# Four small copies per score tile made by ScalarE instead of VectorE, in a kernel whose order a planner writes

## The chip, the cores and the metric

The kernel runs on one core of one Trainium2 chip. The metric is the device time of one launch in microseconds (us). Engines are named as the profile names them: PE is TensorE (PEld its weight load), DVE is VectorE, ACT is ScalarE, POOL is GpSimd, SP is SyncE, which here only issues DMAs.

## What is computed

Attention with pooled queries (4 batches, 8 heads, 1152 keys of 64 values, queries averaged in pairs to 576), and behind it two gated products over 2304 tokens. Everything is float32 at the boundary, the weights come as float64.

```python
def _attn_ref(q, k, v):
    q_pool = q.reshape(B, H, S // factor, factor, D).mean(axis=3)
    scores = scale * np.matmul(q_pool, k.transpose(0, 1, 3, 2))
    scores = scores - np.max(scores, axis=-1, keepdims=True)
    attn = np.exp(scores)
    attn = attn / (np.sum(attn, axis=-1, keepdims=True) + 1e-09)
    return np.matmul(attn, v).astype(np.float32)

def _moe_ref(x, w_in, w_out):              # 512 -> 2048 -> 512
    h = x @ w_in
    return (np.maximum(0.01 * h, h) @ w_out).astype(np.float32)

def _moe2_ref(x, w1, w2, w3, w_out):       # 512 -> 768 (three times) -> 512
    h = np.maximum(np.maximum(x @ w1, x @ w2), x @ w3)
    return (h @ w_out).astype(np.float32)
```

## The kernel before

The program has three stretches. The attention of batch 0 runs first, by one method (`attention`). The attention of batches 1 to 3 runs by another (`attention2`), while PE also does the two products ("experts") of the batch before. When the last attention is done, the experts of batch 3 run alone, together with the 64 tokens of each batch that were set aside.

**A score tile of `attention2`** (`scores2`, L721) holds 64 queries of two heads against all 1152 keys. Each batch has 4 pairs of heads and 9 tiles per pair, so 36 tiles per batch and 108 in all. The keys of one query are cut into quarters: 32 queries sit on 32 partitions four times, so that each quarter of the partitions holds half of the keys of one half of the queries. For one tile there stand in order:

- PE: 16 matmuls into the PSUM tile `s` (the trace has 32 records for them). There is one such tile and one buffer for it, so the next tile's matmuls wait until the last reader of this one is done.
- DVE, L749: one reduce over the tile, which leaves the negated maxima of each partition's keys in two spare columns of `s`.
- L718, in `meet_halves`: four copies of 32 partitions by 2 columns, PSUM to PSUM, that put beside each quarter's maxima those of the quarter that holds the other half of its keys. **These are what the change moves.**
- DVE, L719: a reduce over the two columns, which gives `z`, the joint negated maximum.
- ACT, L752: two exponentials of 576 columns with `z` as bias and their sums accumulated (each with a small accumulator read behind it). They are the last readers of `s`.
- DVE, L756: a transpose in blocks of 32 into `pt`, which the matmuls with the values (`pw`, issued in `values2`, 72 for one half of a pair) read later.

**Other work on the same engines.** PE's expert matmuls write `m` (128x512) and `o` (128x256). ACT takes results out of PSUM (L1107, L1119, L1135, L1157), rounds to the first of two float32r parts (L1042, L826), and while batch 1 runs it also decodes the float64 weights (L963, L966, then L982 to split them); DVE joins the decoded halves (L967), makes parts (L1108) and sums (L1121) and maxima (L1137). POOL makes second parts. The weights are decoded once, in the time of batch 1, and written to DRAM; later batches load them ready.

**What sets the order.** The Python code issues everything in one rough order. Then `plan` (L1172) replays it: it groups instructions into nodes (a score tile's 16 matmuls are one), gives each a `busy` time (how long its engine is taken) and a `late` time (until a reader may start), and walks forward by a list schedule, always taking the node that can begin first. A backward pass sets priorities, up to three times. The order found for each engine is written into the program as fixed; each engine then runs its list strictly in that order. The cost of ACT's nodes, which the change leaves alone, is

```python
late = 185 + 0.8 * cols + 190 * (len(i.outs) > 1) + ...
busy = late - 105
```

with `cols` the columns of the output; a copy of 2 columns is so planned with 82 ns of ACT's time. On DVE a copy of 2 columns was planned with 155 - 80 = 75 ns. Between two nodes of one engine the plan before lets the second start when the first's `busy` time is over, even where it reads the first's result.

Of the kernel before, what the change touches and what calls it, by code (L numbers as in the profile page):

```python
# [23 lines left out]
def kernel(  # L24
# [21 lines left out]
    nc = tc.nc  # L46
# [12 lines left out]
    X0 = 320  # L59
# [655 lines left out]
    def meet_halves(st, z):  # L715
        for c in range(4):
            d = c + 1 - 2 * (c % 2)
            nc.vector.tensor_copy(out=st[32 * c:32 * c + 32, :, 1], in_=st[32 * d:32 * d + 32, :, 0])  # L718
        nc.vector.tensor_reduce(out=z, in_=st, axis=AX.X, op=ALU.min)  # L719

    def scores2(n, ph, i):  # L721
# [271 lines left out]
    ready = set()  # L993
# [51 lines left out]
    class Main:  # L1045
        n = TM
# [11 lines left out]
    class Rest:  # L1058
        n = TR_
# [107 lines left out]
    SEM = 35  # L1167
# [4 lines left out]
    def plan():  # L1172
# [21 lines left out]
        def meet(x, y):  # L1194
            return any(a < d and c < b for a, b in x[2] for c, d in y[2])
# [13 lines left out]
        nodes = []  # L1209
        node_of = {}  # L1210
        for i in todo:
            e = name_of(i.engine)
            key = units.get(i.name)
            out = next((n for n, _ in accesses(i.outs)), None)
# [5 lines left out]
            node_of[i.name] = len(nodes) - 1  # L1220
        count = len(nodes)
        before = [set() for _ in nodes]
        users = {}
        wrote, read = {}, {}
        for n, node in enumerate(nodes):
            for i in node["ins"]:
                for args, others in ((i.ins, (wrote,)), (i.outs, (wrote, read))):
                    for t, ap in accesses(args):
                        users.setdefault(t, set()).add(n)
                        r = region(ap)  # L1230
                        for kind in others:
                            for m, q in kind.get(t, ()):
                                if m != n and m not in before[n] and (nodes[m]["e"] == node["e"] or meet(q, r)):
                                    before[n].add(m)
                        if slots[t][0][0].startswith("ps_") and kind is not None:
                            lo, hi = min(a for a, _ in r[2]) // 512, (max(b for _, b in r[2]) - 1) // 512
                            for m, q in (*read.get(t, ()), *wrote.get(t, ())):
                                if m != n and any(
                                    a // 512 <= hi and lo <= (b - 1) // 512 for a, b in q[2]
                                ):  # L1240
                                    before[n].add(m)
                for args, kind in ((i.ins, read), (i.outs, wrote)):
                    for t, ap in accesses(args):
                        r = region(ap)
                        kind.setdefault(t, []).append((n, r))
# [6 lines left out]
        for n, node in enumerate(nodes):  # L1252
            busy = late = move = 0.0
            for i in node["ins"]:
                outs = [ap for _, ap in accesses(i.outs)]
                cols = size(outs[0].ap) if outs else 512
                op, e = i.opcode, node["e"]
                kind = node["out"].rsplit("_", 1)[0] if node["out"] else ""
                if e == "PE":
                    if kind == "pv":  # L1260
                        one = cols / 1.2
                    elif kind == "pw" and cols >= X0 - 64:
                        one = (cols + 32) / 2.4
                    elif kind == "pw":
                        one = cols / 2.4
                    elif kind == "s" and cols == KQ:
                        one = cols / 4.8
                    elif kind in ("pst", "psf", "psk", "psr"):
                        one = 108.0
                    elif kind == "psq":  # L1270
                        one = max(cols, 64) / 1.2
                    else:
                        one = (cols + 32) / 2.4
                    if n < wide_at:
                        one *= 1.065
                    busy += one * 1.015
                    late = busy + 165
                elif e == "SP":
                    busy = 60.0
                    dst = i.outs[0].bass_ap  # L1280
                    move = size([(0, 1)] + [tuple(x) for x in dst.ap]) * 4 / 330.0
                    if tuple(dst.ap[-1]) == (1, 32):
                        move, busy = 2 * move, 2500.0
                    late = 3000 + move
                elif e == "Activation":
                    late = 185 + 0.8 * cols + 190 * (len(i.outs) > 1) + 180 * (kind[0] == "q" or kind == "kspare") + 100 * (kind == "q") + 85 * (kind in ("wraw", "wsplit"))
                    busy = late - 105
                elif e == "DVE":
                    if op == "TensorReduce":
                        cols = size(next(ap for _, ap in accesses(i.ins)).ap)  # L1290
                    psum = any(slots[t][0][0].startswith("ps_") for t, _ in accesses(i.ins))
                    two = len(list(accesses(i.ins))) > 1 and kind != "p"
                    slow = psum or two or op in ("TensorReduce", "StreamTranspose")
                    late = max(155, 110 + (1.13 if slow else 0.62) * cols + 190 * (kind[0] == "q"))
                    busy = late - 80
                else:
                    late = max(185, 130 + 2.3 * cols)
                    busy = late + 40
            inside = not any(slots[t][0][0].startswith("ps_") for t, _ in accesses(i.ins))
            node["shut"] = node["e"] in ("DVE", "Pool") and inside and i.opcode in (  # L1300
                "TensorTensor", "TensorCopy", "TensorScalarPtr"
            )
            node["busy"], node["late"], node["move"] = busy, late, move
            kind = node["out"].rsplit("_", 1)[0] if node["out"] else ""
            node["mode"] = {"pv": 1, "psz": 1, "pw": 3 * (cols < X0 - 64)}.get(kind, 2 * (kind == "s" and cols == KQ))
# [33 lines left out]
        def lag(n, m):  # L1339
            x, y = nodes[n], nodes[m]  # L1340
            if x["e"] == y["e"]:
                return x["busy"]
            return (3000 + x["move"] if x["move"] else x["late"]) + SEM

        def forward(prio):
# [6 lines left out]
            ready = [0.0] * count  # L1352
# [7 lines left out]
            for _ in range(count):  # L1360
                best = None
                for e in ENGINES:
                    for n in pool[e]:
                        t = max(ready[n], free[e])
                        if nodes[n]["shut"]:
                            t = max(t, shut)
# [50 lines left out]
                        narrow[k] -= 1  # L1417
                        narrow_at[k] = max(narrow_at[k], until[x])
                for m in after[n]:
                    ready[m] = max(ready[m], end + SEM if nodes[m]["e"] != e else t + node["busy"])  # L1420
                    waiting[m] -= 1
                    if not waiting[m]:
                        pool[nodes[m]["e"]].append(m)
# [136 lines left out]
```

## Time and profile before

| what | value |
|---|---|
| device time, median of 3 runs | 1176.5 us (1173.85 to 1178.46) |
| span of the profiled execution, first to last instruction | 1176.8 us |
| stretches of it | attention of batch 0: 0 to 175; batch 1: 175 to 431; batch 2: 431 to 676; batch 3: 676 to 917; join: 917 to 946; experts of batch 3: 946 to 1177 |
| busy in the span | PE 1124.3, DVE 687.6, ACT 541.2, POOL 323.9 us |

The page gives no device time of its own for the profiled execution; its span lies inside the range of the three runs and 0.3 us above their median, so the span is taken as its time. Busy time counts an engine as busy while any instruction of it runs. PE's is a modelled end, so what matters there are the pieces in which it has nothing and waits for another engine.

### The profile page before, as it was taken

The page shows a single profiled execution, that of the slowest core. Times are in us where ns is not written, and L with a number is a line of the kernel's source. Part 1 is how long each engine was busy: PE and PEld are TensorE (multiplying, and loading weights), DVE is VectorE, ACT ScalarE, POOL GpSimd, SP SyncE. Part 2 cuts the span into 40 slices and gives each one's busy share as a digit, 9 for nine tenths or more (in the row PEclk, how much of TensorE's full clock was granted, in tenths as well). Part 3 has the DMA queues.
Part 4 walks back from the last instruction along what each step waited for, and adds up shares of the span by engine and source line. Part 5 has one row for each costly group of instructions (what it writes and reads, how often), then busy time and mean ns, then how long its engine had stood idle before and what let it go on. Part 6 is the DMA issues. An engine that isn't in the chain of part 4 may idle for free. (4 is left out here: it accounts for less than half of the span.)

```text
span 1176.8 us, 28179 instructions
## 1 busy us (share of the span) xinstructions
PE 1124.3 (96%) x11684; PEld 876.7 (75%) x11684; DVE 687.6 (58%) x1412; ACT 541.2 (46%) x1203; POOL 323.9 (28%) x300
## 2 busy tenths in 40 slices
PE   6899999999999899999999989999999999999998
PEld 5566766767767676777777767767677888888898
DVE  5777527888787765776667565875776412222110
ACT  5888788767778633333333333333343221112111
POOL 1111046555554412222311121224111122223110
PEclk9999999999999999999999999999999999999999
DMA  5522069688887976565745483745534533333333
GB/s 171 135 65 66 3 223 308 194 267 274 261 282 225 250 188 175 149 173 144 196 136 164 120 218 121 179 148 147 168 123 146 165 133 127 126 126 123 109 129 105
DMA packets 154875, 193.09 MB, mean 164 GB/s; under 512 B 85500, under 2 KB 115964, under 8 KB 154748
## 3 DMA queue, kind: packets, MB, share of 16 engines
q1 hardware_dynamic: 154748, 191.30, 54.5%
q8 instruction: 92, 1.51, 0.5%
q14 instruction: 35, 0.29, 0.1%
HBM read 153.88 MB, written 35.13 MB: 161 GB/s over the span
## 5 line engine op out<-in xcount | busy, mean ns | idle before, releaser
L136 PE MATMUL m<-x,w 128*128 128x512 f32 x1224 | 293.6, 393 | 0.0
L752 ACT ACTIVATE p<-s,z 128x576 f32<-128x576 f32 x216 | 158.4, 739 | 241.4 <-DVE z L719 200.8
L136 PEld LDWEIGHTS m<-x,w 128*128 128x128 f32 x1224 | 225.3, 188 | 56.2 <-issue 10.2
L756 DVE STREAM_TRANSPOSE pt<-p 128x1152 f32<-128x1152 f32 x108 | 148.7, 1377 | 94.9 <-ACT p L752 94.6
L136 PE MATMUL s<-kt,q 64*32 64x288 f32 (+1 forms) x3568 | 165.0, 408 | 22.3 <-ACT p L752 15.9
L749 DVE TENSOR_REDUCE s<-s 128x2 f32<-128x1152 f32 x108 | 147.6, 1366 | 54.9 <-PE s L136 52.4
L136 PE MATMUL m<-g,w 128*128 128x512 f32 x576 | 141.7, 395 | 1.2 <-POOL g L1109 1.2
L136 PEld LDWEIGHTS s<-kt,q 64*32 64x32 f32 (+1 forms) x3568 | 74.4, 109 | 81.9 <-ACT p L752 37.0
L1109 POOL TENSOR_TENSOR g<-t,g 128x512 fp32r<-128x512 f32 x64 | 85.2, 1333 | 173.1 <-DVE g L1108 170.8
L136 PEld LDWEIGHTS m<-g,w 128*128 128x128 f32 x576 | 104.9, 188 | 30.4 <-issue 6.5
L136 PE MATMUL pw<-pt,v 64*64 64x160 f32 (+1 forms) x3456 | 112.2, 284 | 2.5 <-issue 2.5
L136 PEld LDWEIGHTS pw<-pt,v 64*64 64x64 f32 x3456 | 105.5, 133 | 12.1 <-issue 8.9
L136 PE MATMUL m<-x,wsplit 128*128 128x512 f32 x408 | 103.8, 403 | 0.7 <-ACT t L1135 0.4
L1107 ACT ACTIVATE t<-m 128x512 f32<-128x512 f32 x80 | 44.1, 555 | 120.8 <-PE m L136 113.9
L983 POOL TENSOR_TENSOR wsplit<-wraw,wsplit 128x512 fp32r<-128x512 f32 x56 | 74.2, 1330 | 74.1 <-ACT wsplit L982 48.0
L136 PEld LDWEIGHTS m<-x,wsplit 128*128 128x128 f32 x408 | 75.1, 191 | 23.8 <-issue 6.9
L718 DVE COPY s<-s 32x2 f32<-32x2 f32 x432 | 73.0, 169 | 14.9
L136 PEld LDWEIGHTS m<-pt,w 128*128 128x128 f32 x600 | 76.3, 188 | 4.6 <-DMA pt<-xr 1.0
L136 PE MATMUL m<-pt,w 128*128 128x256 f32 x600 | 77.6, 281 | 1.1 <-DMA pt<-xr 0.6
L1137 DVE TENSOR_TENSOR t<-m,t 128x512 f32<-128x512 f32 (+1 forms) x60 | 37.8, 630 | 69.2 <-PE m L136 69.2
L1108 DVE CAST g<-t 128x512 fp32r<-128x512 f32 x64 | 30.5, 481 | 73.3 <-ACT t L1107 73.2
L780 POOL TENSOR_TENSOR rd<-rh,fold 128x640 fp32r<-128x640 f32 (+1 forms) x24 | 29.9, 1246 | 138.4 <-DVE rh L777 131.2
(142 smaller groups left out, 1372.7 us busy)
## 6 DMA issues: line engine op xcount, KB each, us to landing
w<-w SPq DMA_DIRECT2D x168, 512.0 KB, 3.5
w<-wsplit SPq DMA_DIRECT2D x56, 512.0 KB, 6.0
wraw<-in_moe_w_out_dram SPq DMA_DIRECT2D x22, 512.0 KB, 5.7
wraw<-in_moe_w_dram SPq DMA_DIRECT2D x18, 512.0 KB, 5.3
v<-in_v_dram SPq DMA_DIRECT2D x32, 288.0 KB, 4.4
wraw<-in_moe_w_in_dram SPq DMA_DIRECT2D x16, 512.0 KB, 6.5
v<-in_v_dram SPq DMA_DIRECT2D x10, 576.0 KB, 8.0
qraw<-in_q_dram SPq DMA_DIRECT2D x32, 144.0 KB, 4.5
```

Source lines behind the costliest of these rows:

```text
L136: mm = f(*args, **kwargs)
L718: nc.vector.tensor_copy(out=st[32 * c:32 * c + 32, :, 1], in_=st[32 * d:32 * d + 32, :, 0])
L749: nc.vector.tensor_reduce(out=st[:, :, 0], in_=every, axis=AX.XY, op=ALU.max, negate=True)
L752: nc.scalar.activation(out=p[:, 2 * h:2 * h + 2], in_=ps[h][:, :, 0:KQ], func=ACTF.Exp, bias=z[:, h:h + 1], accum_out=rs[:, h, i:i + 1],)
L756: nc.vector.transpose(out=pt[:, :, i].rearrange("p m h j -> p h m j"), in_=p.rearrange("p (h x) (m i) -> p h (x m) i", h=2, m=KT),)
L780: nc.gpsimd.tensor_tensor(out=rd.rearrange("p (u j) -> p u j", j=nj), in0=rh.bitcast(F32).unsqueeze(2).to_broadcast([128, nu, nj]), in1=se ...
L983: nc.gpsimd.tensor_tensor(out=t[:, 1], in0=r, in1=t[:, 0], op=ALU.subtract)
L1107: nc.scalar.activation(out=t, in_=ps[:, 0:k.n], func=ACTF.Prelu, alpha=0.01)
L1108: nc.vector.tensor_copy(out=gt[:, 0], in_=t)
L1109: nc.gpsimd.tensor_tensor(out=gt[:, 1], in0=t, in1=gt[:, 0], op=ALU.subtract)
L1137: nc.vector.tensor_tensor(out=t, in0=ps[:, 0:k.n], in1=t, op=ALU.max)
```

## The change

In `meet_halves` the four copies are issued to ACT. In the planner four things differ: (a) two nodes of one engine other than PE, of which the second reads what the first wrote, are now `chained`: the second starts only when the first's `late` time and the 35 ns of a semaphore are over; (b) DVE's `late` and `busy` are altered a little, and nodes under 16 columns take 85 ns; (c) the narrow matmuls with the values take 58 or 66.5 ns each (before: 53.3 and 66.7); (d) a price of 200 ns for copies into `s` stands in DVE's branch, where after the change no such copy is left. All 11684 matmuls and all other instructions are the same; their order is planned anew on all engines.

```diff
     def meet_halves(st, z):
         for c in range(4):
             d = c + 1 - 2 * (c % 2)
-            nc.vector.tensor_copy(out=st[32 * c:32 * c + 32, :, 1], in_=st[32 * d:32 * d + 32, :, 0])
+            nc.scalar.copy(out=st[32 * c:32 * c + 32, :, 1], in_=st[32 * d:32 * d + 32, :, 0])
         nc.vector.tensor_reduce(out=z, in_=st, axis=AX.X, op=ALU.min)
...
+                                if args is i.ins and m != n and nodes[m]["e"] == node["e"] != "PE" and meet(q, r):
+                                    chained.add((m, n))
...
                     elif kind == "pw":
-                        one = cols / 2.4
+                        one = (58.0 if cols < X0 // 2 else 66.5)
...
-                    late = max(155, 110 + (1.13 if slow else 0.62) * cols + 190 * (kind[0] == "q"))
-                    busy = late - 80
+                    late = max(160, 110 + (1.09 if slow else 0.62) * cols + 190 * (kind[0] == "q"))
+                    busy = late - 78
+                    if kind == "s" and op == "TensorCopy":
+                        busy = 200.0
+                    elif cols < 16:
+                        busy = 85.0
...
             if x["e"] == y["e"]:
-                return x["busy"]
+                return x["late"] + SEM if (n, m) in chained else x["busy"]
...
-                    ready[m] = max(ready[m], end + SEM if nodes[m]["e"] != e else t + node["busy"])
+                    ready[m] = max(ready[m], end + SEM if nodes[m]["e"] != e or (n, m) in chained else t + node["busy"])
```

The lists of the two programs, engine by engine, show what the new plan does. First PE, in the first part of batch 2: what stands between one score tile (`s`) and the next. `m` are expert matmuls of 512 columns. Before:

```order
L136 MATMUL s<-kt,q 32x288 x16
L136 MATMUL m<-g,w 128x512 x18
L136 MATMUL s<-kt,q 32x288 x16
L136 MATMUL m<-g,w 128x512 x15
L136 MATMUL m<-x,w 128x512 x3
L136 MATMUL s<-kt,q 32x288 x16
```

After:

```order
L136 MATMUL s<-kt,q 32x288 x16
L136 MATMUL m<-x,w 128x512 x21
L136 MATMUL s<-kt,q 32x288 x16
L136 MATMUL m<-g,w 128x512 x18
L136 MATMUL s<-kt,q 32x288 x16
L136 MATMUL m<-g,w 128x512 x21
L136 MATMUL s<-kt,q 32x288 x16
```

Where 18 matmuls stood between two tiles there are now mostly 21.

Next DVE, at neighbouring places of batch 2: one tile before,

```order
L749 TENSOR_REDUCE s<-s 128x2
L718 COPY s<-s 32x2 x4
L719 TENSOR_REDUCE z<-s 128x2
L1121 TENSOR_TENSOR acc<-m,acc 128x512
L756 STREAM_TRANSPOSE pt<-p 128x2x18x32
L1121 TENSOR_TENSOR acc<-m,acc 128x512
```

and two tiles after:

```order
L749 TENSOR_REDUCE s<-s 128x2
L666 STREAM_TRANSPOSE qt<-qraw 128x576
L719 TENSOR_REDUCE z<-s 128x2
L825 TENSOR_TENSOR xf<-pw,rz 128x5x32 x2
L663 STREAM_TRANSPOSE kt<-kraw 128x1152
L756 STREAM_TRANSPOSE pt<-p 128x2x18x32
L1137 TENSOR_TENSOR t<-m,t 128x512
L749 TENSOR_REDUCE s<-s 128x2
L719 TENSOR_REDUCE z<-s 128x2
```

The copies are gone from DVE's list; in their place stands nothing (45 of the 108 tiles) or other work, which `z` then stands behind.

Last ACT, in batch 1, where the weights are decoded. Before:

```order
L752 ACTIVATE p,sums<-s,z 128x576 x2
L982 CAST wsplit<-wraw 128x512
L963 ACTIVATE wraw<-wraw 128x512
L966 ACTIVATE wraw<-wraw 128x512
L982 CAST wsplit<-wraw 128x512
L963 ACTIVATE wraw<-wraw 128x512
L966 ACTIVATE wraw<-wraw 128x512
L752 ACTIVATE p,sums<-s,z 128x576 x2
```

After:

```order
L718 COPY s<-s 32x2 x4
L1107 ACTIVATE t<-m 128x512
L982 CAST wsplit<-wraw 128x512
L752 ACTIVATE p,sums<-s,z 128x576 x2
L963 ACTIVATE wraw<-wraw 128x512
L1107 ACTIVATE t<-m 128x512
L982 CAST wsplit<-wraw 128x512
L966 ACTIVATE wraw<-wraw 128x512
L963 ACTIVATE wraw<-wraw 128x512
L966 ACTIVATE wraw<-wraw 128x512
L718 COPY s<-s 32x2 x4
L752 ACTIVATE p,sums<-s,z 128x576 x2
```

ACT now has two places in each tile's chain, and its other work is planned between them, on either side.

## Rows read from the trace of the kernel before

**Rows 1.** The page: busy time by engine, and the granted TensorE clock in 40 slices.

```profile
PE 1124.3 (96%) x11684; PEld 876.7 (75%) x11684; DVE 687.6 (58%) x1412; ACT 541.2 (46%) x1203; POOL 323.9 (28%) x300
...
PEclk9999999999999999999999999999999999999999
```

**Rows 2.** Busy time by stretch: start:end length, PE PEld DVE ACT POOL, clock, DMA.

```profile
0.00:175.00 175.00, 154.52 (x1007) 112.73 (x1007) 105.45 (x224) 138.73 (x321) 35.27 (x59) 0.99 0.38 109
175.00:431.00 256.00, 243.66 (x2970) 181.50 (x2974) 200.70 (x392) 185.74 (x382) 126.07 (x96) 0.99 0.81 250
431.00:676.00 245.00, 239.35 (x3020) 180.65 (x3019) 162.20 (x348) 83.99 (x198) 53.96 (x45) 1.00 0.58 161
676.00:917.00 241.00, 232.37 (x2886) 173.88 (x2885) 164.04 (x343) 86.67 (x204) 52.13 (x44) 1.00 0.55 156
...
946.00:1177.00 231.00, 226.82 (x1380) 203.26 (x1379) 44.81 (x79) 38.68 (x82) 51.28 (x51) 1.00 0.37 124
```

**Rows 3.** What PE waited for (us, times, longest), batches 1, 2 and 3.

```profile
PE s L136 <- ACT p L752: 7.0, 6, 1.9
PE o L136 <- DVE t L1137: 3.1, 1, 3.1
...
PE s L136 <- ACT p L752: 3.3, 8, 0.7
...
PE s L136 <- ACT p L752: 5.7, 13, 0.8
```

**Rows 4.** Chain that ended last, 728 to 748 us: start, length, what.

```profile
728.03 8.41 PE m L136 x36
736.44 1.22 PE s L136 x32
...
737.68 1.38 DVE s L749
...
739.08 0.17 DVE s L718
739.25 0.02 issue
...
739.89 0.17 DVE z L719
...
740.09 1.57 ACT p L752 x4
...
741.70 1.20 PE s L136 x32
```

**Rows 5.** Timeline of one tile in batch 3: start, length, instruction, idle before.

```profile
773.28 4.37 PE L136 MATMUL m<-g,w 128*128 128x512 f32 x18
...
775.14 0.78 DVE L718 COPY s<-s 32x2 f32<-32x2 f32 x4
...
776.21 0.74 ACT L752 ACTIVATE p<-s,z 128x576 f32<-128x576 f32 x1 [3.30 <-DVE z L719]
776.85 0.19 ACT L752 ACTIVATION_READ_ACCUMULATOR p<-s,z 128x1 f32 x1
776.94 0.73 ACT L752 ACTIVATE p<-s,z 128x576 f32<-128x576 f32 x1
...
777.82 1.21 PE L136 MATMUL s<-kt,q 64*32 64x288 f32 x32 [0.17 <-ACT p L752]
```

**Rows 6.** Groups by shape on ACT: busy us, mean ns, idle before and releaser.

```profile
L963 ACT ACTIVATE wraw<-wraw 128x512 f32<-128x512 f32 x56 | 38.5, 688 | 11.2 <-DMA wraw<-in_moe_w_out_dram 6.0 <-DMA wraw<-in_moe_w_dram 3.2 <-DMA wraw<-in_moe_w_in_dram 2.0
...
L1157 ACT COPY osb<-o 128x256 f32<-128x256 f32 x36 | 13.1, 375 | 26.6 <-PE o L136 26.5 <-ACT x L826 0.2
...
L686 ACT COPY kt<-psq 64x128 f32<-64x128 f32 x8 | 2.1, 259 | 0.1
```

**Rows 7.** Timeline of DVE in batch 1, 238 to 246 us.

```profile
239.92 1.67 DVE L967 SCALAR_TENSOR_TENSOR wraw<-wraw 128x512 int32<-128x512 int32 x1
241.62 1.37 DVE L749 TENSOR_REDUCE s<-s 128x2 f32<-128x1152 f32 x1
```

More of the change, by code (lines that the diff above doesn't have):

```diff
@@ L1222, in plan @@
         before = [set() for _ in nodes]
+        chained = set()
         users = {}
```

## The prediction

> **What bounds the kernel now.** I read the busy times first. PE runs 1124.3 of 1176.8 us, DVE 687.6, ACT 541.2, and the granted clock is nine tenths or more in every slice [rows 1]: PE sets the time, with little left to gain. The same by stretch [rows 2] shows where that little lies: PE has nothing running for 20.5 us before 175 us (no score tile of the changed kind is there), 12.3 in batch 1, 5.7 in batch 2, 8.6 in batch 3; behind 946 us only 4.2, the last output's way out. So all that the change can win lies in 26.6 us, apart from what a new order does by chance to the first stretch.
>
> What PE waits for in those three stretches [rows 3] is mostly one thing: the next score tile's matmuls wait for the exponentials (ACT p) that free the one `s` buffer, 7.0 + 3.3 + 5.7 = 16.0 us. One other wait is large, 3.1 us in batch 1 for a maximum of DVE.
>
> The chain that ended last shows a tile without disturbance [rows 4]. Its matmuls end at 736.44 + 1.22 = 737.66; reduce, four copies (739.08 to 739.87, 0.17 to 0.19 each with 0.02 between), second reduce from 739.89, two exponentials from 740.09, next tile's matmuls at 741.70. So PE must have **4.04 us** of other work between two tiles or it stands. One expert matmul takes 8.41 / 36 = 0.234 us [rows 4], so the usual filling of 18 is worth 4.2 us: it covers the chain with 0.16 us to spare. In the tile of [rows 5] 18 matmuls ran 773.28 to 777.65 and the next tile began at 777.82, idle 0.17 for the exponentials. Any small delay in such a gap is paid by PE.
>
> **The change, part by part.**
>
> *DVE loses the copies.* From the first reduce's end (737.68 + 1.38 = 739.06) to the second's start DVE's list was held for 0.83 us [rows 4]; times 108 tiles, 90 us leave its queue. DVE was busy 78% of batch 1 and 66 and 68% of the others [rows 2], so this is no bound that gives way; it helps where a reduce is late because DVE is still at other work. Such a place is [rows 7]: the reduce of 241.62 began when a decode step of 1.67 us was over, and it is next to the 1.9 us that is the longest wait of [rows 3]. I count nothing for this apart from the waits below.
>
> *ACT gets them.* No copy of 2 columns ran on ACT. A PSUM copy of 256 columns took 375 ns, one of 128 took 259 [rows 6]; drawn on to 2 columns that is an estimate of 145 ns, the low end. The accumulator read, ACT's smallest step here, took 190 ns [rows 5]; 200 is the high end. I take 170, between the two nearest rows. In the new list the second, third and fourth copy each wait for ACT's own semaphore, that is for the copy before; I take the 0.02 us that dependent copies had between them on DVE [rows 4]. Four are then 0.64 to 0.86 us, taken 0.74. Two changes of engine come in: z to the exponential is 0.03 us in [rows 4], and in [rows 5] 0.10 (copies end 775.92, the second reduce needs 0.02 + 0.17, the exponential starts at 776.21); two are 0.06 to 0.20, taken 0.12. Together 0.70 to 1.06, taken 0.86 against 0.83 now. **The chain itself stays about as long**: 4.07 us, bounds 3.91 to 4.27. No row excludes either sign.
>
> *The plan gives PE more between the tiles.* With the durations above (o, of half the columns, at half) I sized each of the 107 gaps between tiles from the two lists. Under 4.5 us (mostly 18 matmuls) lie 17, 21 and 24 gaps of batches 1, 2, 3 before, and 12, 7 and 7 after; the commonest filling is now 21, worth 4.9 us. Against a chain of 4.07 that spares 0.8. I let the 16.0 us of waits shrink with the number of tight gaps: batches 2 and 3 from 9.0 to 9.0 x 14/45 = 2.8, a gain of **6.2**; batch 1 from 7.0 to 7.0 x 12/17 = 4.9, a gain of **2.1**. Even at the upper bound 4.27 a filling of 4.9 covers the chain; at 4.27 the tight gaps cost 26 x 0.1 = 2.6 us, no more than is kept here.
>
> *ACT's list in batch 1.* There ACT was busy 185.7 of 256 us [rows 2], and gets 36 x 4 x 0.19 = 27 us more (24 to 32): 83%, the fullest engine but PE. Summing each tile's ACT work (decode steps of some 0.57 us from start to start, by the 688 of [rows 6] less the overlap of 0.10 seen in [rows 5]) against its PE work, ACT's side is the longer one in 13 of 36 tiles, by 8.4 us in all; before in 4, by 1.3. If no neighbour with room takes anything up this costs 7.1 us, if all do, nothing; 23 tiles have room, so I take a third: **2.4 lost**.
>
> *The single wait of 3.1 us* is DVE being late at the end of batch 1, with copies in front of what PE needs. I let half go: **1.5**. *First stretch:* no copy is there; the new order could move some of its 20.5 idle us either way, taken 0, bounds 3 each way, about the size of its neighbour's one large wait.
>
> Sum: -6.2 - 2.1 + 2.4 - 1.5 = -7.4, so 1176.8 - 7.4 = 1169.4 for the profiled execution; the median of the runs is 0.3 below its span, so **1169**.
>
> **The rivals.**
>
> *Nothing measurable.* The chain was covered anyway (4.04 under 4.2), and what PE waits for moves to ACT: the whole 7.1 us in batch 1, and the 3.1 stays. -6.2 - 2.1 + 7.1 = -1.2: 1175. For it speaks that DVE is nowhere full [rows 2] and that the copies' own path gets no shorter. By the Trainium skill, Perfetto Trace Analysis, section Optimizing Scalar/DVE Operations, moving work from DVE to Scalar may pay if DVE is saturated. By that rule it would not pay here, as the trace has DVE at 66 to 78%. Against it: the gaps in PE's list are wider whatever the copies cost.
>
> *Slower: ACT's fixed order in batch 1.* Copies and exponentials both stand behind decode work now. From the exponentials' end to the next reduce's end there are about 1.2 + 1.4 = 2.6 us [rows 4]; in the new list ACT's other steps there, at the durations used above, are longer than that at 22 of the 36 tiles, by 19 us in all, and each such excess delays the copies. The planner prices a copy at 82 ns of ACT where I expect 190, 0.43 us too little per tile, and a decode step can itself wait for its DMA (11.2 us in all [rows 6]) with the score chain behind it. If all 19 are paid, less the 8.3 and 1.5 won elsewhere: 1186. It decides from about 16 us lost in batch 1. Against it: 19 gaps there hold 4.9 us or more, 0.8 over the chain, and ACT keeps 17% free.
>
> *Faster still: copies that overlap on ACT.* In [rows 5] the second exponential starts 0.09 us after the accumulator read in front of it, which lasts 0.19. If the copies ran like that, four would take 0.17 + 3 x 0.09 = 0.44, the chain 3.77, and of the 7.7 us of waits left above I would let half go: 1165. Against it stand the waits on ACT's own semaphore. By the Trainium skill, ScalarE: Activation LUTs, section What ACT_TABLE_LOAD costs, ACTIVATEs that follow each other overlap by about 93 ns. The row agrees for steps without a wait; no row shows it for steps with one.
>
> **How the numbers follow.** A measurement of this kernel can tell about 0.5%, 5.9 us, from no change: faster means under 1170.6. The forecast gets 0.45; its own spread of some 4 us (bounds of the first stretch, of the third taken for ACT) lies on that line, so 0.33 of it counts as faster and 0.12 as the same. Overlapping copies 0.10, faster. Nothing measurable 0.29. Slower 0.16. That makes 0.43 faster, 0.41 the same, 0.16 slower. The range takes in the fast rival with 6 us for a good turn of the first stretch and of the single waits, 1159, and ends at 1182, which leaves out most of the slow one.
>
> **What the next profile would show.** Right: the four copies on ACT at 0.15 to 0.20 us each, one after the other; the time from the first reduce's end to the second's start within 0.70 to 1.06; waits of PE for the exponentials under 4 us in batches 2 and 3 together; DVE some 70 us less busy, ACT some 75 more. Wrong: copies of 0.25 or more, or long steps of DVE or ACT in the chain (second reduce behind a transpose, exponentials behind a decode step) that raise a tile's 4.04 above 4.9, so that the new filling no longer covers it; or waits of PE in batch 1 of 20 us and more.

## The result, and the profile after

The changed kernel takes **1158.35 us** (median of five runs, 1157.2 to 1161.12) against 1176.5 before (five runs, 1173.85 to 1180.4): a ratio of 0.985, with a 95% interval of 0.9832 to 0.9868. The forecast was 1169, a gain of 7.4; it gained 18. The direction and the place were right, the size was less than half.

The page of the kernel after: busy time, granted clock, the chain that ended last by engine, the first reduce and the copies.

```profile
PE 1120.2 (97%) x11684; PEld 879.7 (76%) x11684; DVE 616.4 (53%) x980; ACT 599.1 (52%) x1635; POOL 323.6 (28%) x300
...
PEclk9899999999999999999999999999999999999999
...
PE 61%; ACT 1%; DVE 1%; issue 1%; DMA 0%; SPq 0%; ACTq 0%
...
L749 DVE TENSOR_REDUCE s<-s 128x2 f32<-128x1152 f32 x108 | 147.1, 1362 | 41.4 <-PE s L136 40.5
...
L718 ACT COPY s<-s 32x2 f32<-32x2 f32 x432 | 55.1, 128 | 180.0 <-DVE s L749 161.1
```

Against [rows 1] DVE has lost 71.2 us and ACT gained 57.9. The granted clock is 1.00, the level of 2.4 GHz, throughout batches 1 to 3, where batch 1 had 0.99 before ([rows 2] and the rows below); in the first stretch one slice shows 8 tenths instead of 9. The chain that ended last is now PE's own at nearly every step: ACT and DVE hold 1% of the span each. The span fell from 1176.8 to 1156.6, by 20.2; PE's idle time fell from 52.5 to 36.4 (span less busy), by 16.1, and its busy time by 4.1. (The device time of a run is some 1.8 above its span, 1158.35 for 1156.6 here, so the execution profiled before was one of 1178.5; by medians the gain is 18.2. The prediction took its span as its time; the 7.4 taken from 1178.5, less the 2.0 down to the median, would have given the same 1169.)

Where the idle time went shows in the same windows as [rows 2], batches 1 to 3 (start:end length, PE PEld DVE ACT POOL, clock, DMA):

```profile
174.60:414.90 240.30, 230.48 (x2859) 169.67 (x2862) 177.08 (x242) 200.88 (x514) 128.58 (x97) 1.00 0.84 260
414.90:644.80 229.90, 228.46 (x2871) 172.33 (x2868) 141.80 (x206) 105.67 (x347) 51.47 (x43) 1.00 0.62 167
644.80:897.00 252.20, 250.15 (x3152) 194.11 (x3151) 140.79 (x215) 109.72 (x357) 55.36 (x47) 1.00 0.56 159
```

PE idles 9.8, 1.4 and 2.05 us here, 13.3 in all, against 12.3, 5.7 and 8.6, 26.6 in all. The three batches take 722.4 us instead of 742.0, for nearly the same matmuls (8882 records against 8876; the cuts between batches don't fall on the same matmul, so single lengths are not compared). Everything outside them lost only 0.6.

PE's waits for the exponentials in the kernel after (us, times, longest), batch 1 and batch 2; batch 3 has none:

```profile
PE s L136 <- ACT p L752: 6.7, 14, 0.8
PE m L136 <- ACT t L1107: 1.6, 1, 1.6
...
PE s L136 <- ACT p L752: 0.5, 2, 0.3
```

In [rows 3] they were 7.0, 3.3 and 5.7. In batch 1 the sum has stayed, though the long ones are gone: fourteen of at most 0.8 stand where six of up to 1.9 stood. In batches 2 and 3 9.0 us have become 0.5. The wait of 3.1 us for L1137 is gone too.

A tile of batch 2 after, timeline (start, length, instruction, idle before):

```profile
541.90 1.20 PE L136 MATMUL s<-kt,q 64*32 64x288 f32 x32
...
543.03 5.05 PE L136 MATMUL m<-x,w 128*128 128x512 f32 x21
543.21 1.37 DVE L749 TENSOR_REDUCE s<-s 128x2 f32<-128x1152 f32 x1 [0.53 <-PE s L136]
...
544.66 0.60 ACT L718 COPY s<-s 32x2 f32<-32x2 f32 x4 [2.68 <-DVE s L749]
545.30 0.16 DVE L719 TENSOR_REDUCE z<-s 128x2 f32<-128x4 f32 x1 [0.72 <-ACT s L718]
...
545.50 0.74 ACT L752 ACTIVATE p<-s,z 128x576 f32<-128x576 f32 x1 [0.23 <-DVE z L719]
546.14 0.19 ACT L752 ACTIVATION_READ_ACCUMULATOR p<-s,z 128x1 f32 x1
546.23 0.73 ACT L752 ACTIVATE p<-s,z 128x576 f32<-128x576 f32 x1
...
546.85 0.20 ACT L752 ACTIVATION_READ_ACCUMULATOR p<-s,z 128x1 f32 x1
...
548.01 0.68 PE L136 MATMUL s<-kt,q 64*32 64x288 f32 x11
```

The first reduce ends at 544.58, the copies run 544.66 to 545.26, the second reduce starts at 545.30: 0.72 us from reduce to reduce, where DVE alone took 0.83 [rows 4]. Over all tiles, by the start and end of each record, the median from reduce to reduce went from 0.85 to 0.73 us in batches 2 and 3, and from the second reduce to the exponential from 0.095 to 0.035. In batch 1 there is no such gain, as the next rows show. The exponentials with their reads end at 547.05, and PE, filled by 21 matmuls, comes back to `s` at 548.01: over 0.9 us of slack, where the filling of 18 had 0.16.

Batch 1 after, ACT's timeline, shows what its fixed order costs there:

```profile
233.28 0.60 ACT L718 COPY s<-s 32x2 f32<-32x2 f32 x4
233.81 0.66 ACT L963 ACTIVATE wraw<-wraw 128x512 f32<-128x512 f32 x1
234.49 0.74 ACT L752 ACTIVATE p<-s,z 128x576 f32<-128x576 f32 x1
```

The same stretch on DVE:

```profile
231.42 1.35 DVE L749 TENSOR_REDUCE s<-s 128x2 f32<-128x1152 f32 x1
232.68 0.67 DVE L1121 TENSOR_TENSOR acc<-m,acc 128x512 f32<-128x512 f32 x1
233.92 0.16 DVE L719 TENSOR_REDUCE z<-s 128x2 f32<-128x4 f32 x1 [0.56 <-ACT s L718]
```

The reduce is over at 232.77, but the copies begin at 233.28, behind ACT's decode steps; `z` is ready at 234.08, but the exponential begins at 234.49, behind L963. That is 0.5 + 0.4 us of delay in one tile, of the kind that the slower rival feared. It is the rule there: from the first reduce's end to the first exponential the 36 tiles of batch 1 take 1.62 us on average, against 1.17 before, which is 16 us in all. (Batches 2 and 3 take 1.09 and 1.08, against 1.12 and 1.17.)

### The profile page after: what moved, and what is told of

Same layout as the page of the kernel before. It is cut to its first block, busy times and chain, and to the rows that moved or that the text cites. A ratio compares the mean times of both kernels' runs of the same rounds, so it can differ in the third digit from the quotient of the medians.

```text
span 1156.6 us, 28296 instructions
## 1 busy us (share of the span) xinstructions
PE 1120.2 (97%) x11684; PEld 879.7 (76%) x11684; DVE 616.4 (53%) x980; ACT 599.1 (52%) x1635; POOL 323.6 (28%) x300
## 4 chain that ended last, share of the span: by engine, by line
PE 61%; ACT 1%; DVE 1%; issue 1%; DMA 0%; SPq 0%; ACTq 0%
PE m L136 41%; PE pw L136 7%; PE s L136 7%; PE o L136 6%; ACT p L752 1%; DMA pt<-xr 0%; DVE s L749 0%; ACT s L718 0%; PE psr L136 0%; DVE pt L756 0%; ACT t L1107 0%; SPq L1005 0%; ACT osb L1157 0%; DVE z L719 0%; DVE t L1137 0%
## 5 line engine op out<-in xcount | busy, mean ns | idle before, releaser
L136 PEld LDWEIGHTS m<-x,w 128*128 128x128 f32 x1224 | 225.5, 188 | 57.5 <-issue 10.2
L136 PE MATMUL s<-kt,q 64*32 64x288 f32 (+1 forms) x3568 | 161.7, 409 | 11.5 <-ACT p L752 7.2
L718 ACT COPY s<-s 32x2 f32<-32x2 f32 x432 | 55.1, 128 | 180.0 <-DVE s L749 161.1
L1137 DVE TENSOR_TENSOR t<-m,t 128x512 f32<-128x512 f32 (+1 forms) x60 | 37.7, 629 | 74.1 <-PE m L136 73.2
L1043 POOL TENSOR_TENSOR y<-t,y 128x512 fp32r<-128x512 f32 x24 | 30.9, 1289 | 139.8 <-ACT y L1042 139.7
```

Of the source, the lines that this page charges most:

```text
L136: mm = f(*args, **kwargs)
L718: nc.scalar.copy(out=st[32 * c:32 * c + 32, :, 1], in_=st[32 * d:32 * d + 32, :, 0])
L1043: nc.gpsimd.tensor_tensor(out=t[:, 1], in0=src, in1=t[:, 0], op=ALU.subtract)
L1137: nc.vector.tensor_tensor(out=t, in0=ps[:, 0:k.n], in1=t, op=ALU.max)
```

## The experiments

Two causes could carry the gain: the **room** (the new plan leaves more matmuls between two tiles) and the **move** (DVE rid of the copies, a shorter exchange), and beside them the **luck** of one order against another, since each edit makes the planner write all lists anew. "Tight" counts the gaps between tiles, of 107, that hold under 4.5 us of PE's work, from the lists, as in the prediction. "Waits" are PE's waits for the exponentials, "idle" the span less PE's busy time, both of the profiled execution; (a) to (d) are the parts of the planner's change.

| kernel | copies on | plan | median us | ratio to before, 95% | tight | waits | idle |
|---|---|---|---|---|---|---|---|
| before | DVE | before's | 1176.5 | 1 | 62 | 15.9 | 52.5 |
| after | ACT | corrected | 1158.35 | 0.985 (0.9832-0.9868) | 26 | 7.2 | 36.4 |
| e1 | DVE | corrected | 1167.31 | 0.994 (0.992-0.9961) | 29 | 10.2 | 41.1 |
| e2 | ACT | before's | 1157.82 | 0.9859 (0.9837-0.9881) | 29 | 8.1 | 37.1 |
| e3 | ACT | (a) only | 1159.07 | 0.9869 (0.9844-0.9894) | 27 | 6.5 | 36.9 |
| e4 | ACT | (b), (c), (d) | 1163.71 | 0.9911 (0.9891-0.9932) | 28 | 12.5 | 43.1 |
| e5 | ACT, DVE loaded | corrected | 1162.19 | 0.9887 (0.9859-0.9914) | 24 | 7.5 | 41.9 |
| e6 | DVE in batch 1 | corrected | 1162.82 | 0.9897 (0.9875-0.9918) | 23 | 3.0 | 39.5 |
| e7 | ACT, dearer | corrected | 1161.24 | 0.9879 (0.985-0.9908) | 31 | 7.8 | 36.9 |
| e8 | ACT, twice | corrected | 1174.76 | 1.0 (0.9986-1.0015) | 26 | 19.1 | 50.4 |
| e9 | DVE, twice | before's | 1219.77 | 1.0391 (1.0361-1.0421) | 62 | 49.5 | 86.8 |
| e10 | DVE | before's, SEM 40 | 1175.94 | 0.9999 (0.9978-1.0021) | 59 | 15.9 | 50.7 |
| e11 | DVE | (a) only | 1189.47 | 1.0124 (1.0096-1.0152) | 40 | 20.6 | 56.6 |
| e12 | ACT | corrected, SEM 40 | 1161.09 | 0.9881 (0.9853-0.9909) | 36 | 5.6 | 36.8 |
| e13 | ACT | before's, tiles first | 1173.51 | 0.9982 (0.9963-1.0002) | 69 | 16.3 | 48.0 |
| e14 | DVE | before's, tiles 800 ns later | 1182.85 | 1.0067 (1.0046-1.0088) | 22 | 4.1 | 52.2 |
| e15 | none | corrected | 1154.29 | 0.9824 (0.9785-0.9864) | 32 | 4.1 | 33.9 |
| e16 | ACT | corrected, tiles 300 ns later | 1166.24 | 0.9914 (0.9886-0.9942) | 24 | 2.2 | 42.4 |
| e17 | ACT | as after | 1156.92 | 0.9835 (0.9809-0.9862) | 26 | 8.6 | 37.0 |
| e18 | ACT | as e2 | 1157.39 | 0.9841 (0.9812-0.987) | 29 | 8.3 | 38.4 |

### The change taken apart

e1 is the kernel after with the copies back on DVE:

```diff
-            nc.scalar.copy(out=st[32 * c:32 * c + 32, :, 1], in_=st[32 * d:32 * d + 32, :, 0])
+            nc.vector.tensor_copy(out=st[32 * c:32 * c + 32, :, 1], in_=st[32 * d:32 * d + 32, :, 0])
```

> Copies stay on DVE, all the planner's corrections are in. Counted in the lists, 29 of 107 gaps between score tiles hold under 4.5 us of PE work (62 before, 26 in the changed kernel). Theory W (the time went with the number of tight gaps, whoever makes the copies): most of the gain, 1160 to 1165 us, as the tight gaps left are a little shorter than in the changed kernel. Theory D (what counts is that DVE is freed of 0.83 us per tile and the chain is 0.1 us shorter): little of the gain, 1170 to 1176. Theory P (the corrections alone do it): 1157 to 1161.

It took 1167.31 us. The tight gaps are nearly as few as after (29), the waits 10.2, longest 1.7. The corrections without the move gain 7.2 us on its series' 1174.54, in this one order. It is not the plan's room alone that is measured so: with (a) the planner also puts other work of DVE between the reduce and the copies, and from the first reduce's end to the first exponential the tiles take 1.62, 1.41 and 1.30 us on average in batches 1 to 3, against 1.17, 1.12 and 1.17 before.

e2 is the kernel before with only that line changed the other way, the planner untouched:

> Copies on ACT, the planner as before. The lists have 29 tight gaps again, though no price was corrected: the two changes of engine in the chain make the plan leave more room. Theory W: 1158 to 1163. Theory D: 1157 to 1161, as all that counts is in. Theory P: little of the gain, 1170 to 1176.

1157.82 us, as fast as the whole change, and tight in 29 gaps. So the room comes with the move alone. The planner's code shows a reason: it prices the exchange on DVE at 4 x 75 = 300 ns from the reduce's `busy` end to the second reduce, and on ACT at 80 (what the reduce's `late` is beyond its `busy`) + 35 + 3 x 82 + 187 + 35 = 583. It plans 283 ns more for an exchange that on the chip takes 0.11 us less.

e3 has ACT's copies with (a) alone, e4 with all but (a):

```diff
-                                    chained.add((m, n))
+                                    pass
```

> Copies on ACT, of the corrections only that dependent nodes of one engine wait for the full latency; prices as before. 27 tight gaps, three of them in batch 3 shorter than 4.1 us. Theory W: 1158 to 1164. Theory D: 1157 to 1161. Theory P splits: 1158 if this correction carries the gain, 1168 or more if the prices do.

> Copies on ACT, of the corrections only the prices; dependent nodes of one engine are planned with the busy time again. 28 tight gaps. Theory W: 1158 to 1163. Theory D: 1157 to 1161. Theory P splits the other way: 1158 if the prices carry the gain, 1168 or more if the full latency does.

1159.07 and 1163.71. No part of the corrections adds to what e2 has; (b) to (d) without (a) even lose 5.9 against e2, in one order. To be sure of it, after and e2 ran again side by side:

> The changed kernel once more, beside the next one on the same chip: 1156 to 1161.

> Copies on ACT, planner as before, once more. If the corrections add nothing: within 3 us of the changed kernel; if they carry part of the gain: 5 us and more above it.

1156.92 and 1157.39, ratios 0.9835 and 0.9841 with intervals that cover each other: **with the copies on ACT the corrections add nothing that can be measured.**

### Luck of the order

Two kernels change only the planner's price of a semaphore, which alters every list a little:

```diff
-    SEM = 35
+    SEM = 40
```

> The kernel before with one number of the planner altered that means nothing here, the price of a semaphore 40 instead of 35 ns, to see how far a new order alone moves the time with the copies on DVE. 59 tight gaps of 107. If orders scatter by chance as much as the move gained, anything from 1158 to 1190; if not, within 4 us of the kernel before.

> The changed kernel with the same meaningless number altered, 40 instead of 35 ns. 36 tight gaps. If the gain belongs to the copies on ACT: 1157 to 1164. If it was the luck of one order: up to 1176.

Before so altered takes 1175.94, after 1161.09. e11 gives the kernel before (a) alone:

> Copies on DVE, of the corrections only the full latency between dependent nodes. 40 tight gaps, those of batches 1 and 2 as many as before, batch 3 four. If moving the copies off DVE is what counts, it stays with the other kernels that have them there: 1166 to 1176. If scatter of orders is as large as the gain, it can fall among those with the copies on ACT, 1157 to 1163.

1189.47, slower than before: the waits rise to 20.6, and fewer tight gaps (40) did not help. The exchange itself has become longer, as in e1 and more so: with other work of DVE between reduce and copies, or between copies and second reduce, the median from reduce to reduce is 1.17 us, where before has 0.85. And the clock fell: batches 1 and 2 of its profile have four stretches at 1.2 GHz, 20.5 us together, each at or right behind a wait of PE of 1.7 to 2.2 us. At half speed they can cost up to 10 us, an estimate. e7 plans ACT's copies at what they cost on the chip (`busy, late = 160.0, 165.0`):

> The changed kernel, with the copies on ACT planned at what they take (160 ns of ACT each from start to start, where the plan had 82). If the plan's ignorance of 0.3 us per tile makes the waits of batch 1, 1152 to 1156; if ACT's load itself makes them, or the gaps' room covers the error, 1157 to 1160.

1161.24: a truer price gives nothing. Orders scatter by up to 6 us with ACT's copies (1157.8 to 1163.7) and by 22 with DVE's (1167.3 to 1189.5), and the count of tight gaps does not rank them. Yet of the plain variants none with DVE's copies is under 1167 (before, e1, e10, e11), and those with ACT's lie between 1157 and 1164 (after, e2, e3, e4, e7, e12). (e13 and e16 below, which shift the tiles in the plan, lie above.) That there is a gain is no luck of one order; its size holds to some 6 us. Part of the scatter may be the clock: in batches 1 to 3 the profiles of before, e1, e4, e5, e6, e9 and e13 have one stretch at 1.2 GHz and e16 has two, each behind a wait of PE of 1.3 to 3.6 us; after, e2, e3, e7, e8, e10, e12, e14, e15, e17 and e18 have none.

### How much room there is

e8 and e9 make the four copies twice in batches 2 and 3, the second four at no price, so that PE's list stays as it is; in after on ACT, in before on DVE. PE's instructions stand in the same order in the traces of e8 and after, and in those of e9 and before, so no luck of the order comes in:

```diff
+        for again in range(2 if n >= 2 * NP else 1):
...
+                if again:
+                    unpriced.add(extra.ins.name)
...
+            if node["ins"][0].name in unpriced:
+                busy = late = 0.0
```

> The changed kernel with the four copies made twice in batches 2 and 3, the second four planned at no cost, so that the order on PE is that of the changed kernel and the chain of 72 tiles is longer by some 0.63 us. If the room that the lists show is real (gaps of 21 matmuls, 4.9 us, against a chain of 4.0), only the tight gaps pay: summed over the list 6.7 us, so 1164 to 1167. If there is no such room and every tile's delay is paid: 72 x 0.63 = 45 us, over 1195.

> The kernel before, with the four copies on DVE made twice in batches 2 and 3, the second four planned at no cost: the order on PE is that of the kernel before, the chain of 72 tiles is longer by some 0.78 us. It is the same test of room as with the copies on ACT, which cost 16 us there. If the kernel before had no room in its gaps of 18 matmuls, the sum over its list gives 37 us for a chain of 4.9 against 4.4 for one of 4.1: some 32 us more than before, 1202 to 1212. If room is not what sets the kernels apart, it costs the same 16 us as on ACT, about 1190.

After gets 16.4 us slower, before 43.6; both more than expected. ACT's timeline in e8 shows the doubled exchange:

```profile
548.66 1.24 ACT L721 COPY s<-s 32x2 f32<-32x2 f32 x8 [2.60 <-DVE s L754]
```

It adds 0.64 us per tile, 46 over 72 tiles, of which after pays about a third. On DVE four more copies are 0.78 us [rows 5], 56 over 72 tiles, of which before pays over three quarters. PE's waits in e8 (us, times, longest):

```profile
PE s L136 <- ACT p L757: 19.1, 36, 1.3
```

and in e9:

```profile
PE s L136 <- ACT p L757: 49.5, 52, 1.9
```

So the spare time per gap, which the prediction set against the chain, is real, and it is the best founded of the causes here: it takes up most of an added delay after, and little of it before. Not all of e9's loss need be the chain, though: DVE also has 45 us more to do there, and the waits grew by 33.6 of the 43.6 us.

e13 keeps ACT's copies and takes room away: before's planner, but a score tile goes ahead of all other work of PE.

```diff
-                            k = (t + WAIT * bool(stay), prio[n], n)
+                            k = (t + WAIT * bool(stay), prio[n] - 1e5 * (nodes[n]["mode"] == 2), n)
```

> Copies on ACT, planner as before but for one rule: a score tile goes on PE before any other work that could start at the same time. In the lists 69 of 107 gaps are tight again (11, 29, 29 by batch). If the room in the gaps is what the move gained: back towards before, 1167 to 1174, with waits for exponentials of 8 us and more in batches 2 and 3. If DVE's relief gained it: 1157 to 1162.

1173.51, with 69 tight gaps (11, 29 and 29 by batch): nearly the whole gain is gone. PE's largest waits in it:

```profile
PE s L136 <- ACT p L752: 16.3, 27, 2.1
```

12.6 of them fall in batch 1, against 6.7 after, though its tight gaps are no more than after (11 against 12): there the chain is longer, 1.84 us from the first reduce's end to the first exponential instead of 1.62. Batches 2 and 3 have 3.7 in 58 tight gaps, where before had 9.0 in 45 [rows 3] and after has 0.5 in 14. So without room the move still saves waits there, and the room that was taken away explains only 3.2 of the 15 us by these waits. The run does not show that room alone carries the gain.

The opposite, room with the copies on DVE: before with every tile held back by 800 ns.

```diff
-                            t = max(t, nsmallest(c + 1, rooms[group])[-1][0])
+                            t = max(t, nsmallest(c + 1, rooms[group])[-1][0] + (800 if nodes[n]["mode"] == 2 else 0))
```

> Copies on DVE, planner as before but for one number: the buffer of score tiles is planned free 0.8 us later than computed. In the lists 22 of 107 gaps are tight (7, 6, 9), fewer than in the changed kernel, and summed over the gaps only 0.5 us is missing for a chain of 4.1. If room is what counts: 1157 to 1163 without any move of the copies. If DVE's load is what counts: 1168 to 1176.

1182.85, slower than before, with only 22 tight gaps. PE's waits in e14:

```profile
PE psr L136 <- ACT p L752: 10.7, 10, 3.3
...
PE s L136 <- ACT p L752: 4.1, 6, 1.8
```

The waits at the tiles did fall, to 4.1, but 10.7 us for the same exponentials stand elsewhere, at the sums behind the tiles, half of them after 645 us, as do others of up to 1.5 us. The ten stand all along the three batches, and the longest, 3.3, comes right behind the last tile, at 934 us. So room without the move does take away the waits at the tiles, but this order pays for it elsewhere, and the run doesn't tell what room alone is worth. e16 does the same to after, by 300 ns:

> The changed kernel with the buffer of score tiles planned free 0.3 us later. 24 tight gaps (5, 10, 9); for a chain of 4.1 us 0.4 us is missing over all gaps, most of it gone from batch 1. If tight gaps still make waits in batch 1: 1152 to 1156, better than the changed kernel. If those waits come from ACT's full list: 1157 to 1161.

1166.24: waits for the exponentials only 2.2, and yet 8 us slower than after, with a new one of 3.6 (`o` for L1137) and 3.9 at the matmuls with the values, for which the profile names no cause. In its tiles, too, PE is held up more often (8.5 us against 1.7 after; what this is stands in the account of the prediction below). More room than the planner gives is no gain in this order.

### What DVE's relief is worth

e5 gives DVE the load back, but off the chain: after with one more reduce per tile, of the exponentials, whose result nobody uses.

```diff
+        zz = st_p.tile([128, 2], F32, tag="zz", bufs=1, name="zz")
+        nc.vector.tensor_reduce(out=zz[:, 0:1], in_=p[:, 0:2], axis=AX.XY, op=ALU.max)
```

> The changed kernel with one more DVE instruction per tile: a reduce over 576 columns of the exponentials into a spare tile, some 0.7 us, planned with its price, read by nobody and not in the chain of score tiles (its result isn't used; the output is the same). It gives DVE back the load that the copies took off it, with the chain as short as in the changed kernel. If DVE's occupancy is what counted (theory D1), the 9 us between the corrected plan with copies on DVE and the changed kernel come back: 1164 to 1169. If it is the path through ACT that counted (theory D2: the chain is shorter and plans around it are looser), 1157 to 1161.

DVE is busy for 685.8 us, as before (687.6), and the kernel takes 1162.19: 3.8 us above after, no more than orders scatter, and 13 below its series' 1175.23. So DVE's load as such is not what most of the gain comes from, and whether it has a price at all isn't shown.

e6 has the copies on DVE in batch 1, where ACT is fullest, and on ACT in the others:

```diff
+            move = nc.vector.tensor_copy if n < 2 * NP else nc.scalar.copy
```

> Copies on DVE in batch 1, on ACT in batches 2 and 3, corrected plan. ACT is at 200.9 of 240.3 us in batch 1 of the changed kernel and PE waited there 7.0 us for exponentials. If ACT's full list makes those waits, they fall and the kernel beats the changed one: 1151 to 1156. If DVE is the scarcer engine there also (D1), batch 1 gets longer: 1161 to 1166.

1162.82, slower than after by some 4. PE's waits in it:

```profile
PE pw L136 <- issue: 3.5, 3, 1.7
PE m L136 <- DVE acc L1122: 3.1, 3, 1.9
...
PE s L136 <- ACT p L753: 3.0, 8, 0.5
```

The waits for the exponentials shrink to 3.0, as one would hope with ACT's list relieved, but expert matmuls now wait for DVE's sums. The difference is no more than orders scatter, so where batch 1's copies are better off stays open.

e15 leaves out the exchange of maxima (each quarter of the partitions uses its own), to show what is left to win at this place:

```diff
-        for c in range(4):
-            d = c + 1 - 2 * (c % 2)
-            nc.scalar.copy(out=st[32 * c:32 * c + 32, :, 1], in_=st[32 * d:32 * d + 32, :, 0])
-        nc.vector.tensor_reduce(out=z, in_=st, axis=AX.X, op=ALU.min)
+        nc.vector.tensor_copy(out=z, in_=st[:, :, 0])
```

> The changed kernel without the four copies: each quarter of the partitions takes its own maximum as z, so that the exponentials of the two halves of a query's keys have different biases. What is left out is the exchange of maxima. If copies on ACT cost nothing any more where they are: 1155 to 1160. If their place in the chain or on ACT still costs: 1145 to 1153.

1154.29: of the 22 us between before and a kernel with no copies, the change has taken 18, and 4 are left, by one order each. No version that computes the whole beat after and e2 clearly.

## Why the prediction was right in kind and too small

**Right: what bounds the kernel, and where the gain lies.** PE with its waits for the exponentials sets the time; the waits of batches 2 and 3 fell below 4 us, as its last part asked (0.5). The slack of the gaps has its part in this: e8 and e9 show it taking up an added delay.

**Right: the exchange.** It was to run one copy after the other, 0.70 to 1.06 us from reduce to reduce; it took 0.72. Overlapping copies (0.44) did not come: 0.60 is four steps of about 0.16 with a wait for ACT's own semaphore between them. What was mis-sized is the single copy: "200 is the high end. I take 170", and 145 the low end; it takes 128 ns, below both. So the taken 0.86 was too long, and "The chain itself stays about as long" is off in batches 2 and 3: the median from the first reduce's end to the first exponential fell from 1.11 and 1.13 to 0.92 us. In batch 1 it rose, by 0.45 us on average. In a gap with 0.16 to spare 0.2 us is much: e13 has 0.06 us of waits per tight gap of batches 2 and 3 (3.7 / 58), before had 0.20 (9.0 / 45); how much of it is the exchange and how much DVE's shorter list isn't separated.

By the Trainium skill, Perfetto Trace Analysis, section Optimizing Scalar/DVE Operations, an access to PSUM costs ScalarE less per instruction (about 51 ns) than VectorE (about 125). The prediction weighed that section's rule on a saturated DVE and missed this sentence. The trace agrees in sign: 128 ns on ACT against 0.17 to 0.19 us on DVE [rows 4]. That section's other sentence, that such a move may pay if DVE is saturated, does not say that it can't pay otherwise, as the prediction's rival read it: DVE was busy 58% [rows 1], and the move alone (e2) gained 1.4%.

**Right in the sum, the terms not shown: batch 1.** Forecast were 2.1 less for the wider gaps and 2.4 more for ACT's list, together 0.3 more of waits; found are 7.0 before and 6.7 after. No run separates the two terms, so that the sum fits may be luck.

**The step that failed: "So all that the change can win lies in 26.6 us".** It took PE's idle time in the three batches for all that could be won there, and put the busy time at nothing. But busy time fell by 6.3 us, a third of the 19.6 that the batches lost, and the largest part of what the forecast lacks. The rest of the miss is three terms of idle time that were mis-sized:

| batches 1 to 3 | forecast | found |
|---|---|---|
| waits for the exponentials, from 16.0 | -5.9 (-6.2 - 2.1 + 2.4) | -8.8 (to 7.2) |
| the wait of 3.1 for L1137 | -1.5 | -3.1 |
| PE's other idle time, from 7.5 | 0 | -1.4 (to 6.1) |
| PE's busy time | 0 | -6.3 (715.4 to 709.1) |

The wait for L1137 went whole, not by half: "I let half go" had no row behind it. The waits of batches 2 and 3 were to shrink with the number of tight gaps, to 2.8, but 0.5 are left: with the shorter chain the 14 that remain mostly cover it too.

Half of the busy time's part, 3.2 us, are the score matmuls themselves (133.8 to 130.6 us for all 3456). In most tiles they start within 0.80 us, from the first to the last. Before, seven tiles took 1.0 to 2.6 us, 6.0 us too much in all; after, only two did, 1.7 us. One of the seven (before):

```profile
370.28 0.67 PE L136 MATMUL s<-kt,q 64*32 64x288 f32 x2
371.23 1.20 PE L136 MATMUL s<-kt,q 64*32 64x288 f32 x30 [0.28 <-ACT kt L696]
```

PE stops for 0.95 us between two starts, for keys that ACT still copies; the profile counts 0.28 of it as idle and the rest as busy, because a matmul's end is modelled. So a busy PE hid waits. The move has no visible part in this: by kernel the excess and the busy time of the score matmuls go together (1.4 and 131.3 us in e13, 1.7 and 130.6 after, 2.1 and 131.9 in e1, 3.7 and 133.0 in e2, 6.0 and 133.8 before, 8.5 and 135.0 in e16), whoever makes the copies and however many gaps are tight. These 4.3 us, 3.2 of them counted as busy, look like luck of the order. So may the 3.1 for L1137 be: e1 and e2 have no such wait, e10 has 1.8 and e16 3.6.

Another piece is the clock. Before, in batch 1:

```profile
245.69 1.21 PE L136 MATMUL s<-kt,q 64*32 64x288 f32 x32 [1.93 <-ACT p L752]
...
246.80:250.30 3.50, 3.50 (x17) 0.51 1.06 345
```

PE has stood for 1.93 us, waiting for exponentials, and just behind this the granted clock is 0.51, that is 1.2 GHz: seven matmuls of 512 columns start 0.43 us apart and not 0.23, and 1.4 us are lost as busy time. So this wait cost more than its length. It is not so behind every wait: the 3.1 us for L1137 had no such stretch behind it, nor did a wait of 1.8 us at the same place in e10. After, batches 1 to 3 have no such stretch. The remaining 1.7 us of the busy time **stay open**.

"I count nothing for this apart from the waits below", said of DVE's relief, is not refuted, nor shown. The reduce does begin earlier, on average 0.62 us after the start of its tile's last matmul instead of 0.75, but no run separates what PE gains by it, and e5 finds no price of DVE's load beyond the scatter of orders. That e1 gains 7.2, nearly the 7.4 forecast, is luck: it is one order of kernels that lie between 1167 and 1189, and its exchange is longer than before. How the gain splits between room, shorter exchange and DVE's relief **stays open**; shown is that the move as a whole makes it (e2), and that gaps with slack take up delays (e8 against e9).

**The rivals.** "Nothing measurable" leaned on a chain covered anyway, and on all 7.1 us of ACT's excess being paid; neither came. "Slower" had its mechanism, and nearly its size: where it summed 19 us of delay on ACT in batch 1, 16 came. But PE's waits there did not rise (7.0 and 6.7): the gaps were wider, and the reduces began 0.17 us earlier on average. "Faster still", 1165, came nearest in size, for a reason that did not occur.

## What to carry to other kernels

On an engine that is 96% busy, look at each gap's slack against the chain that must fit into it, and not at the average load of the helpers: with 0.16 us to spare an added 0.78 per tile was paid to over three quarters, with more to spare an added 0.64 to about a third. Don't take the bounding engine's busy time as a floor: compare the starts of its instructions, and its clock behind long waits. A small PSUM copy on the path may be cheaper on ACT than on DVE even with two changes of engine, as long as ACT's list is not full: in batch 1 the path got longer. And where a planner writes the order, test a move and a new price apart: here the move made the room by itself, and the prices, truer as they were, gave nothing.

## What the runs showed of the hardware beyond that

Copies of 32 partitions by 2 columns within PSUM take 128 ns on ACT, and about 0.16 us from start to start where each waits for the one before; e8's eight in 1.24 us say the same. On DVE, before, they take 169 ns and 0.195 from start to start (0.78 for four [rows 5]). The changes of engine cost little where the next engine stands idle, as in the tile of batch 2 above: 0.08 us from DVE's reduce to ACT's first copy, 0.04 from the last copy to the second reduce, 0.04 from there to the exponential.

```profile
L718 DVE COPY s<-s 32x2 f32<-32x2 f32 x432 | 73.0, 169 | 14.9
```
